# A table of places for every step of a recurrence-and-mixing kernel, and two edits to its gate arithmetic

## The chip, the cores and the metric

The kernel runs on one core of one Trainium2 chip. The metric is the device time of that core in microseconds (us), lower is better. Its engines work side by side, each through its own queue in order: TensorE (PE, with its weight loads PEld), VectorE (DVE), ScalarE (ACT), GpSimd (POOL) and SyncE (SP), which issues the DMAs.

## The reference

Two stages. The first is a complex, gated linear recurrence for 4 batches x 8 heads x 768 positions x 48 channels; the second mixes each position with the one before it and sends it through three matrix products.

```python
mag = np.sqrt(a_re * a_re + a_im * a_im)
scale = np.minimum(mag, 0.999) / (mag + 1e-06)
a_re_n, a_im_n = a_re * scale, a_im * scale
for t in range(S):                       # S_re, S_im: 48 x 48 for each batch and head
    new_re = ar * S_re - ai * S_im
    new_im = ar * S_im + ai * S_re
    S_re, S_im = new_re + k[t] v[t]^T, new_im
    y[t] = q[t] @ S_re
x_prev = x shifted by one position       # x: y with the heads side by side, 384 wide
xk = mu_k * x + (1 - mu_k) * x_prev      # xr likewise, with mu_r
k = np.maximum(xk @ w_k, 0)              # 384 -> 1024
v = k * k @ w_v                          # 1024 -> 384
out = sigmoid(xr @ w_r) * v
```

## The kernel before, in words

The work is cut into 8 units: unit `u` is one half (384 positions) of batch `u // 2`. Each unit passes three stages.

- **`gate(u)`** turns the gate into a running logarithm and a running angle. It loads `g` (the rows a_re, a_im, k, q, 128 channels at a time, three times) and `v`. `a0` takes |a_re| on ACT (line 591), a guard that sums how far a_re lies under a least value (line 595), Ln, Exp(-ln) and, on DVE, the ratio a_im / a_re (line 604). `a1` makes the logarithm of the magnitude, `a2` scans it along the positions (line 637) and multiplies k and q by its exponentials (line 654). `b0` takes the arctangent, scans the angle (line 665) and brings it to -pi..pi in a tile `r`: a product that is stored as a whole number (line 682), the remainder (685), a clamp (688) and, by clearing the sign bit, its absolute value (691). `b1` takes cosine and sine on ACT and multiplies k and q by them (line 704: "the rotations", six for a unit).
- **`attend(u)`**: PE turns the rotated k and q (line 768), forms the state's growth (789), which DVE adds up (800, 802), the scores (818), which DVE masks (823), and the values `y` (849); ACT copies from PSUM (774, 871). SP moves the rotated rows into the stacked buffers `kq` (736) and `y` into the tile `xt` (882).
- **`mix(u)`**: DVE and ACT form `xm` (348, 356) and split it into a high and a low half `x` (364, 367). PE multiplies by the weights (line 381: 3 blocks `z` for the sigmoid and 8 for w_k, of 9 matmuls each); ACT takes relu and square (418, 422), DVE splits the square (`hhi`, 426; `hlo`, 430), and PE multiplies by w_v (line 444: 8 blocks `o` of 9). DVE multiplies by the sigmoid (460).

The weights come as doubles in 10 pieces (`fetch`) and are turned into two float halves (`convert`): ACT (506, 526), four DVE steps (509, 512, 516, 520) and one POOL subtraction (529) for each piece, through two buffers `wx`.

All this is first recorded as steps and then ordered by the class `Plan`. Each recorded instruction group has an engine, a cost, what it reads and writes, and the buffer slots it uses. `Plan.run` plays a clock forward: whenever an engine is free, it takes, of the steps that are ready and whose slots are free, the one that is due first. The order so found is the order in which the program is written out, so each engine's queue is fixed when the program is built. Before, the due times come from `due`: each step is given a time (`AT_A`, `AT_M`, `AT_M0`, `DELAY`: so many units after the unit's beginning), PE's costs are summed in that order, and all else is counted back from PE.

The buffers that matter here: `g` has two (units u and u + 2 share one), `m`, `ph`, `sq`, `xk`, `xr`, `xt`, `zr` and the accumulators `o` have one, `kq` six, PSUM five blocks. The tile `r` of units 0 and 1 lies in the mixing buffer `xk` (`R_XK = 2`), that of later units in `sq`.

Of the kernel before, what the change touches and what calls it, by code (L numbers as in the profile page):

```python
# [69 lines left out]
class Plan:  # L70
# [21 lines left out]
    def op(self, engine, cost, emit, reads=(), writes=(), uses=(), table=None, heat=1.0):  # L92
# [5 lines left out]
        for k in writes:  # L98
# [12 lines left out]
    def due(self):

        ops = self.ops
        late = [math.inf] * len(ops)
        t = 0.0
        for i in sorted((i for i, o in enumerate(ops) if o["engine"] == "PE"), key=lambda i: (ops[i]["at"], i)):
            t += ops[i]["cost"]
            late[i] = t
        left = [len(f) for f in self.follow]
        due, free = [0.0] * len(ops), {}  # L120
        heap = []

        def push(i):
            late[i] = min(late[i], t + 2.0)
            heapq.heappush(heap, (-late[i], -i))
        for i, n in enumerate(left):
            if not n:
                push(i)
        while heap:
            i = -heapq.heappop(heap)[1]  # L130
            o = ops[i]
            e = o["engine"]
            s = late[i] - o["cost"]
            if e not in ("PE", "NONE"):
                s = min(late[i], free.get(e, math.inf)) - o["cost"]
                free[e] = s
                if e == "SP":
                    s -= self.START + self.ARRIVE
            due[i] = s
            for j in o["after"]:  # L140
                late[j] = min(late[j], s - self.LATENCY)
                left[j] -= 1
                if not left[j]:
                    push(j)
        return due

    def run(self):
# [33 lines left out]
        while len(order) < len(ops):  # L181
# [868 lines left out]
```

## Time and profile before

| | |
|---|---|
| time, median of 3 runs | 477.33 us (476.31 to 477.69) |
| the profiled execution's own time | 476.16 us |
| its span, first to last instruction | 474.40 us |
| instructions in the span | 12425 |
| granted TensorE clock, mean | 0.938 |
| read from HBM, written | 31.07 MB, 4.72 MB |

The profile's page gives for each engine the time in which it was busy. Its strip of 40 slices (11.9 us each) shows the busy share in tenths, and in the row PEclk the clock that TensorE was granted. The views used below are: the table of stretches (busy time of every engine between two moments), the groups of instructions by line and shape (count, total busy time, mean ns of one, then idle time before them), one line's own view (shortest, median and longest instruction), the waits (who waited for whom), and the timeline (start, duration, and in brackets the idle time before and what ended it). A group's durations overlap a little with their neighbours, so a sum of them is somewhat above busy time.

### The profile page before, as it was taken

Reading aid. Unit: us, or ns where it says so; the run is one execution under the profiler, and the core shown is the slowest. Engines: PE = TensorE matmul, PEld = TensorE weight load, DVE = VectorE, ACT = ScalarE, POOL = GpSimd, SP = SyncE. Lnnn points to the kernel's source line nnn. Section 1 sums busy time; section 2 is a strip of 40 time slices with the busy share of each in tenths; the row PEclk is TensorE's granted clock in tenths of the full one; section 3 lists DMA queues with packets and bytes.
Section 4 is the critical chain, followed back from the end, with each engine's and each line's share of the span. In section 5 each row is a group of like instructions: output and inputs, shape, how many; then the busy total and the mean of one; then the engine's idle time right before and its main releaser. Section 6 shows DMA issues by size and latency. Waiting matters only on the chain.

```text
span 474.4 us, 12425 instructions
## 1 busy us (share of the span) xinstructions
PE 382.8 (81%) x5162; PEld 351.0 (74%) x5162; DVE 374.5 (79%) x610; ACT 299.9 (63%) x498; POOL 32.3 (7%) x45
## 2 busy tenths in 40 slices
PE   0008445879966999979989999999799988999994
PEld 0006433868755999869978898999689967999993
DVE  0798999969989889898989799569967898248222
ACT  7768445597549667957894775866669753434530
POOL 4004210214210000000000000000000000000000
PEclk9999755789978999999999999999899989999998
DMA  8998154502717056416551834072523115210101
GB/s 287 409 409 142 36 184 161 123 1 52 275 26 182 21 195 203 106 51 192 181 130 61 296 102 114 34 252 100 135 78 82 45 48 137 76 35 10 51 0 57
DMA packets 25935, 60.26 MB, mean 127 GB/s; under 512 B 5392, under 2 KB 14608, under 8 KB 25872
## 3 DMA queue, kind: packets, MB, share of 16 engines
q1 hardware_dynamic: 25872, 59.40, 40.7%
q8 instruction: 42, 0.69, 0.6%
q14 instruction: 21, 0.17, 0.1%
HBM read 31.07 MB, written 4.72 MB: 75 GB/s over the span
## 4 chain that ended last, share of the span: by engine, by line
PE 42%; DVE 28%; ACT 13%; DMA 7%; issue 5%; SPq 3%; POOL 1%; DVEq 0%; ACTq 0%
PE z L381 19%; PE o L444 12%; PE y L849 5%; DVE ph L665 4%; DMA kq<-g 3%; PE sc L818 3%; DVE g L654 3%; DMA g<-in_gat 3%; SPq L736 3%; PE up L789 2%; ACT sq L264 2%; DVE m L637 2%; DVE g L704 2%; DVE xm L356 2%; ACT L261 2%
## 5 line engine op out<-in xcount | busy, mean ns | idle before, releaser
L381 PE MATMUL z<-x,w 128*128 128x384 f32 x792 | 155.9, 347 | 5.0 <-DVE state L800 1.9
L381 PEld LDWEIGHTS z<-x,w 128*128 128x128 f32 x792 | 140.3, 193 | 8.4 <-DVE state L800 2.2
L444 PE MATMUL o<-hhi,w 128*128 128x384 f32 x384 | 103.8, 353 | 1.3 <-DVE hhi L426 1.3
L444 PEld LDWEIGHTS o<-hhi,w 128*128 128x128 f32 x384 | 71.3, 196 | 3.2 <-DVE hhi L426 2.5
L444 PE MATMUL o<-hlo,w 128*128 128x384 f32 x192 | 67.9, 354 | 5.6 <-DVE hlo L430 5.5
L768 PE MATMUL tr<-ident,g 128*128 128x128 f32 (+1 forms) x144 | 27.7, 311 | 49.3 <-DVE g L704 47.8
L418 ACT ACTIVATE r<-z 128x384 f32<-128x384 f32 x64 | 31.0, 486 | 55.2 <-PE z L381 55.0
L768 PEld LDWEIGHTS tr<-ident,g 128*128 128x128 f32 (+1 forms) x144 | 17.8, 148 | 55.9 <-issue 31.9
L426 DVE CAST hhi<-h 128x384 fp32r<-128x384 f32 x64 | 22.6, 353 | 33.3 <-ACT h L422 21.2
L704 DVE TENSOR_TENSOR g<-g,r 128x768 f32<-128x768 f32 x48 | 43.7, 951 | 1.8 <-ACT r L264 1.7
L444 PEld LDWEIGHTS o<-hlo,w 128*128 128x128 f32 x192 | 37.8, 197 | 8.7 <-DVE hlo L430 8.6
L818 PE MATMUL sc<-kq 112*64 112x64 f32 x768 | 31.7, 233 | 8.9 <-DMA kq<-g 2.7
L818 PEld LDWEIGHTS sc<-kq 112*64 112x64 f32 x768 | 26.9, 144 | 15.5 <-issue 6.2
L430 DVE TENSOR_TENSOR hlo<-h,hhi 128x384 fp32r<-128x384 f32 x64 | 35.8, 559 | 1.4
L264 ACT ACTIVATE sq<-m 128x1152 f32<-128x1152 f32 (+2 forms) x27 | 28.1, 1054 | 11.1 <-DVE m L620 7.0
L364 ACT CAST x<-xm 128x384 fp32r<-128x384 f32 x48 | 24.2, 511 | 17.1 <-DVE xm L356 13.6
L422 ACT ACTIVATE h<-r 128x384 f32<-128x384 f32 x64 | 33.2, 523 | 2.5 <-DVE hlo L430 1.5
L789 PEld LDWEIGHTS up<-v,kt 64*48 64x48 f32 (+1 forms) x1408 | 27.0, 139 | 6.8 <-ACT kt L774 3.9
L849 PE MATMUL y<-kq,state 112*48 112x64 f32 (+1 forms) x704 | 25.7, 229 | 7.5 <-DVE state L800 5.1
L849 PEld LDWEIGHTS y<-kq,state 112*48 112x48 f32 (+1 forms) x704 | 23.2, 136 | 11.4 <-DVE state L800 5.3
L789 PE MATMUL up<-v,kt 64*48 64x48 f32 (+1 forms) x1408 | 29.4, 231 | 2.4 <-DVE state L800 1.3
L529 POOL TENSOR_TENSOR w<-wx,w 128x768 fp32r<-128x768 f32 (+1 forms) x10 | 24.5, 2454 | 85.6 <-ACT w L526 85.6
(74 smaller groups left out, 551.3 us busy)
## 6 DMA issues: line engine op xcount, KB each, us to landing
kq<-g SPq DMA_DIRECT2D x96, 144.0 KB, 3.2
g<-in_gat SPq DMA_DIRECT2D x18, 768.0 KB, 6.9
raw<-in_w_all SPq DMA_DIRECT2D x9, 768.0 KB, 11.6
g<-in_gat SPq DMA_DIRECT2D x12, 384.0 KB, 7.3
v<-in_vt SPq DMA_DIRECT2D x24, 192.0 KB, 4.6
out_t<-y SPq DMA_DIRECT2D x24, 192.0 KB, 2.1
xt<-ys SPq DMA_DIRECT2D x48, 72.0 KB, 2.2
kq<-g SPq DMA_DIRECT2D x32, 96.0 KB, 2.8
```

The costliest lines, as they stand in the source:

```text
L264: nc.scalar.activation(out=out, in_=in_, func=func, **kw)
L381: nc.tensor.matmul(z, lhsT=wt[s[0]][:, part, s[1]], rhs=r[which][:, ct], start=n == 0, stop=n == 3 * NT - 1)
L418: nc.scalar.activation(out=t["r", j], in_=t["f", j], func=AF.Relu)
L422: nc.scalar.activation(out=t["h", j], in_=t["r", j], func=AF.Square)
L430: nc.vector.tensor_tensor(out=t["lo", j], in0=t["h", j], in1=t["hi", j].bitcast(F32), op=ALU.subtract)
L444: nc.tensor.matmul(tiles["o", mt], lhsT=wt[W_V + 2 * j][:, part, ts(mt, P)], rhs=r, start=j == 0 and n == 0, stop=j == NJ - 1 and n == 2)
L529: nc.gpsimd.tensor_tensor(out=t["w"][:, :, 1], in0=t["x"], in1=t["w"][:, :, 0].bitcast(F32), op=ALU.subtract)
L704: nc.vector.tensor_tensor(out=g[:, ct, 2 * i:2 * i + 2], in0=g[:, ct, 2:4], in1=t["r"][:, ct, 1 - i:2 - i].to_broadcast([P, 2, U]), op=ALU ...
L768: nc.tensor.transpose(out=t["tr", c, part][:, ct * P:(ct + 1) * P], in_=G[u][:, ct, 2 * part, c * P:c * P + rows], identity=ident)
L789: nc.tensor.matmul(t["up", c, s][i * HR:(KR if i else HR), h * D:(h + 1) * D], lhsT=keys[r, i * D:(2 * D if i else HR)], rhs=V[u][c][r, h ...
L818: nc.tensor.matmul(sc[s * SB:s * SB + SB, i, c], lhsT=kq[h][:, 0, q], rhs=kq[h][:, 1, q], start=True, stop=True)
L849: nc.tensor.matmul(t["y", v][s][rows, h // 2 % 2, c], lhsT=lhsT[:, cols], rhs=rhs, start=(s, h % 2) not in begun, stop=stop)
```

## The change

It has three parts.

1. **Places instead of due times.** `Plan.due` now reads a table, `ORDER`: for each part of the work (gate, fetch, convert, attend, mix of each unit) and each engine, one number for each of its steps. Among ready steps with free slots the one with the lowest number goes first. Costs and delays of `Plan`'s clock are altered, and a slot is free only a latency after its last use. Those numbers order the program; none of them is executed.
2. **Gates without the clamped ratio.** |a_re| becomes Relu(a_re), the separate guard (line 595) is gone, and the guard's sum is instead gathered by the Exp that is there anyway. The limits of the final check are set accordingly.
3. **The tile `r`** is laid out with its two halves apart, so that each half of a unit is one run of 1152 numbers and not three runs of 384; its absolute value is taken by ACT and no longer by DVE; and unit 1's `r` lies in `sq`, not in the mixing buffer (`R_XK = 1`).

```diff
-AT_A = (0.0, 0.6)
-AT_M = (1.2, 2.1)
+ORDER = {
+    ("g", 0): dict(SP=(1, 16, 6, 15, 23, 27, 13, 8, 20,), ACT=(11, 47, 49, 61, 16, 31, 10, 45, 46, 26,), DVE=(12, 22,
+         13, 11, 8, 29, 9, 7, 33, 4,)),
...
+    ("w", 0): dict(ACT=(78,), DVE=(72,), POOL=(1,)),
...
-R_XK = 2
+R_XK = 1
...
-    def due(self):
+    def due(self, places):
+        steps = {}
+        for o in self.ops:
+            steps.setdefault((o["key"][0], o["engine"]), set()).add(o["key"][1])
+        place = {}
+        for (phase, e), s in steps.items():
+            given = places.get(phase, {}).get(e, range(len(s)))
+            place.update(((phase, e, x), n) for x, n in zip(sorted(s), given, strict=True))
+        return [place[o["key"][0], o["engine"], o["key"][1]] for o in self.ops]
...
-                    heapq.heappush(ends, (end, i))
+                    heapq.heappush(ends, (end + self.LATENCY, i))
...
-                    nc.scalar.activation(out=t["m"][:, c], in_=G[u][:, c, 0], func=AF.Abs)
-                def low():
-                    nc.scalar.activation(out=t["ph"][:, c], in_=G[u][:, c, 0], func=AF.Relu, scale=-1.0, bias=re_min,
-                                         accum_out=stat[:, i:i + 1])
+                    nc.scalar.activation(out=t["m"][:, c], in_=G[u][:, c, 0], func=AF.Relu)
...
-                op_act(n, lambda: act(t["ph"][:, c], t["m"][:, c], AF.Exp, scale=-1.0), table=(u, "exp"),
-                       reads=kk("m", c), writes=kk("ph", c), uses=[s_m, s_ph])
+                op_act(n + 110, lambda: act(t["ph"][:, c], t["m"][:, c], AF.Exp, scale=-1.0, accum_out=stat[:, i:i + 1]),
+                       table=(u, "exp"), reads=kk("m", c), writes=kk("ph", c), uses=[s_m, s_ph])
...
-                        t["r"] = (mp["x"] if u < R_XK else tp).tile([P, NT, 2, U], F32, tag="xk" if u < R_XK else "sq", name="r")
-                    t["n", c.start] = t["r"][:, c, 1].bitcast(I32)
+                        t["r"] = (mp["x"] if u < R_XK else tp).tile([P, 2, NT, U], F32, tag="xk" if u < R_XK else "sq", name="r")
+                    t["n", c.start] = t["r"][:, 1, c].bitcast(I32)
...
-                op_dve(n, lambda: nc.vector.tensor_single_scalar(
-                    out=t["n", c.start], in_=t["r"][:, c, 0].bitcast(I32), scalar=0x7FFFFFFF, op=ALU.bitwise_and),
-                    rate=2, reads=kk("r0", c), writes=kk("r1", c), uses=[s_r])
+                op_act(n, lambda: nc.scalar.activation(out=t["r"][:, 1, c], in_=t["r"][:, 0, c], func=AF.Abs),
+                       reads=kk("r0", c), writes=kk("r1", c), uses=[s_r])
```

How the queues move is seen at three places; the line numbers of the changed kernel differ from those above. The first is DVE at the start, in `gate(0)`: `m`, `ph`, `g`, `sq` and `stat` belong to the gate, `wx` and `raw` to the weights. Before:

```order
L627 TENSOR_SCALAR m<-m 128x384
L620 SCALAR_TENSOR_TENSOR m<-sq,m 128x768
L637 SCALAR_TENSOR_TENSOR m<-m,sq 128x384
L644 COPY stat<-m 128x1
L627 TENSOR_SCALAR m<-m 128x768
L646 TENSOR_SCALAR m<-m 128x384
L637 SCALAR_TENSOR_TENSOR m<-m,sq 128x384 x2
L654 TENSOR_TENSOR g<-g,sq 128x768
```

Of the change, in the same stretch of DVE's queue:

```order
L638 TENSOR_TENSOR ph<-g,ph 128x768
L671 SCALAR_TENSOR_TENSOR m<-m,sq 128x384
L550 TENSOR_SCALAR wx<-wx 128x384
L678 COPY stat<-m 128x1
L553 TENSOR_SCALAR wx<-wx 128x384
L680 TENSOR_SCALAR m<-m 128x384
L557 SCALAR_TENSOR_TENSOR wx<-raw,wx 128x384
L654 SCALAR_TENSOR_TENSOR m<-sq,m 128x768
L688 TENSOR_TENSOR g<-g,sq 128x768
L561 SCALAR_TENSOR_TENSOR wx<-raw,wx 128x384
```

The conversion of the weights' first piece has moved up between the gate's steps. Counted through DVE's whole queue, four pieces are converted before PE's first `z` block was given its last input before, and seven with the change.

The second place is ACT at the very start (`m` and `ph` of the gate, `tiny` a constant). Before:

```order
L591 ACTIVATE m<-g 128x384
L595 ACTIVATE ph,stat<-g,re_min 128x384
L261 ACT_TABLE_LOAD
L264 ACTIVATE m<-m,tiny 128x384
L591 ACTIVATE m<-g 128x768
L595 ACTIVATE ph,stat<-g,re_min 128x768
L264 ACTIVATE m<-m,tiny 128x768
L264 ACTIVATE ph<-m 128x384
```

Of the change:

```order
L632 ACTIVATE m<-g 128x384
L304 ACT_TABLE_LOAD
L307 ACTIVATE m<-m,tiny 128x384
L307 ACTIVATE ph,stat<-m 128x384
L650 ACTIVATE sq,stat<-ph 128x384
L632 ACTIVATE m<-g 128x768
```

The first third of the gate (128x384) now goes ahead of the other two (128x768), and the guard's instructions are gone.

The third place is DVE where the last unit is rotated (`g_3826` before and `g_3787` after are unit 7's tile; `hhi` and `hlo` belong to the mixing of unit 5, `pt` to the scores, `xm` and `x` to the mixing of unit 6). Before:

```order
L688 TENSOR_SCALAR r_4691<-r_4691 128x3x384
L430 TENSOR_TENSOR hlo_4724<-h_4671,hhi_4708 128x384
L691 TENSOR_SCALAR r_4691<-r_4691 128x3x384
L426 CAST hhi_4738<-h_4693 128x384
L367 TENSOR_TENSOR x_4673<-xm_4621,x_4673 128x384
L430 TENSOR_TENSOR hlo_4742<-h_4693,hhi_4738 128x384
L356 SCALAR_TENSOR_TENSOR xm_4744<-dx_4639,mu_sb_81,xt_4325 128x384
L704 TENSOR_TENSOR g_3826<-g_3826,r_4691 128x768
L426 CAST hhi_4758<-h_4726 128x384
L704 TENSOR_TENSOR g_3826<-g_3826,r_4691 128x768
L430 TENSOR_TENSOR hlo_4765<-h_4726,hhi_4758 128x384
L704 TENSOR_TENSOR g_3826<-g_3826,r_4691 128x768 x4
```

Of the change:

```order
L722 TENSOR_SCALAR r_4482<-r_4482 128x1152
L467 CAST hhi_4533<-h_4460 128x384
L471 TENSOR_TENSOR hlo_4536<-h_4460,hhi_4533 128x384
L737 TENSOR_TENSOR g_3787<-g_3787,r_4482 128x768
L467 CAST hhi_4565<-h_4502 128x384
L737 TENSOR_TENSOR g_3787<-g_3787,r_4482 128x768
L856 TENSOR_TENSOR pt_4581<-sc_4552,mask_71 128x384
L471 TENSOR_TENSOR hlo_4583<-h_4502,hhi_4565 128x384
L737 TENSOR_TENSOR g_3787<-g_3787,r_4482 128x768 x2
L467 CAST hhi_4637<-h_4632 128x384
L737 TENSOR_TENSOR g_3787<-g_3787,r_4482 128x768
```

The absolute value (line 691) has left DVE, one row of `x` and three of `xm` fewer stand ahead of the last rotation, and 45 instead of all 48 `hlo` steps of units 0 to 5.

More of the change, by code (lines that the diff above doesn't have):

```diff
@@ L102, in op, with steps, run @@
         self.ops.append(dict(engine=engine, cost=cost, emit=emit, after=after - {None, i}, uses=uses,
-                             at=self.at, table=table, heat=heat))
-    def steps(self, steps, a, b):
+                             key=self.key, table=table, heat=heat))
+    def steps(self, steps, phase):
         for i, f in enumerate(steps):
-            self.at = a + (b - a) * (i + 0.5) / len(steps)
+            self.key = phase, (i + 0.5) / len(steps)
             f()
-    def due(self):
[L113 to L147, printed above, removed]
+    def due(self, places):
[7 more added lines that the diff above has]
+        return [place[o["key"][0], o["engine"], o["key"][1]] for o in self.ops]
+    def run(self, places):
         ops = self.ops
@@ L225, in run @@
                         free[e] = end
-                    for at in (free[e], end):
+                    for at in (free[e], end + self.LATENCY):
                         heapq.heappush(events, at)
-                    heapq.heappush(ends, (end, i))
+                    heapq.heappush(ends, (end + self.LATENCY, i))
                     for j in self.follow[i]:
@@ L236, in run @@
                     o["start"], o["end"], o["on"], o["took"] = t, end, e, o["cost"]
-        self.length = end
+        self.length = max(o["end"] for o in ops)
         for i in order:
@@ L398, in out_ @@
                 nc.scalar.copy(out=zr[u][:, mt], in_=tiles["z", mt])
-            op_pe(1.58, mul, reads=parts(1) + [("w", W_R + ct) for ct in range(NT)], writes=[("z", u, mt)],
+            op_pe(1.62, mul, reads=parts(1) + [("w", W_R + ct) for ct in range(NT)], writes=[("z", u, mt)],
                   uses=[sp, part_slot[1]])
@@ L445, in mul @@
                                          start=j == 0 and n == 0, stop=j == NJ - 1 and n == 2)
-            op_pe(1.58, mul, reads=[("hhi", u, j), ("hlo", u, j), ("w", W_V + 2 * j)] + [("o", u, j - 1)] * (j > 0),
+            op_pe(1.62, mul, reads=[("hhi", u, j), ("hlo", u, j), ("w", W_V + 2 * j)] + [("o", u, j - 1)] * (j > 0),
                   writes=[("o", u, j)], uses=[so, *hs[j]])
@@ L774, in f1 @@
                         nc.scalar.copy(out=t["kt", c][:rows, :, part], in_=t["tr", c, part].rearrange("p (h d) -> p h d", d=D))
-                    op_pe(0.35, f0, heat=0.5, reads=[("kqs" if part else "kqc", u, ct) for ct in range(NT)],
+                    op_pe(0.41, f0, heat=0.8, reads=[("kqs" if part else "kqc", u, ct) for ct in range(NT)],
                           writes=[("tr", u, c, part)], uses=[sp, sk, g_slot[u]])
@@ L917, in tile_kernel @@
         n = range(len(pieces))
-        run(gate(0) + [lambda i=i: fetch(i) for i in n] + [lambda i=i: convert(i) for i in n] + gate(1), 0, 0)
+        run(gate(0), ("g", 0))
+        for i in n:
+            run([lambda i=i: fetch(i)], ("f", i))
+        for i in n:
+            run([lambda i=i: convert(i)], ("w", i))
+        run(gate(1), ("g", 1))
         for u in range(NU):
-            t = u + DELAY if u else 0
-            run(attend(u), t + AT_A[0], t + AT_A[1])
-            a, e = AT_M if u else AT_M0
-            run(mix(u), t + a, t + e)
+            run(attend(u), ("a", u))
+            run(mix(u), ("m", u))
             if u + 2 < NU:
-                run(gate(u + 2), 0, 0)
+                run(gate(u + 2), ("g", u + 2))
         with tc.manual_schedule():
-            plan[0].run()
+            plan[0].run(ORDER)
     bad = keep.tile([1, 1], I32, name="bad")
@@ L1010, in tile_kernel @@
                 zr.clear()
-                plan[0].steps(mix(u), 0, 1)
-                plan[0].run()
+                plan[0].steps(mix(u), ("m", u))
+                plan[0].run({})
 def kernel(q, k, v, a_re, a_im, moe_mu_k, moe_mu_r, moe_w_k, moe_w_v, moe_w_r):
```

112 lines of the change are left out of this document (86 added, 26 removed).

## The prediction

> **What bounds the kernel now.** I read the page's strip first, then cut the span into stretches by what PE does, then looked at the waits inside each. In the strip a digit is the busy share of 11.9 us in tenths.
>
> ```profile
> PE   0008445879966999979989999999799988999994
> DVE  0798999969989889898989799569967898248222
> PEclk9999755789978999999999999999899989999998
> ```
>
> The order of saturation is the point: DVE is full from the second slice on while PE is empty or half idle until about slice 13; from slice 32 on PE is full and DVE falls off. The stretches (columns: length, then busy us of PE, PEld, DVE, ACT, POOL, then the granted clock, the DMA engines' share and their GB/s) are cut at PE's first transpose, its first `z` block, the transposes of unit 2 and the end of the dense part:
>
> ```profile
> 0.00:31.70 31.70, 0.00 (x0) 0.03 (x1) 17.87 (x33) 21.22 (x34) 5.73 (x21) 1.00 0.95 365
> 31.70:88.30 56.60, 30.57 (x649) 24.82 (x649) 55.10 (x76) 33.56 (x52) 9.50 (x5) 0.73 0.54 151
> 88.30:141.80 53.50, 45.34 (x461) 41.33 (x461) 47.36 (x68) 34.97 (x55) 15.20 (x6) 0.87 0.29 91
> 141.80:320.00 178.20, 167.95 (x2505) 155.01 (x2506) 153.54 (x258) 131.77 (x219) 0.87 (x2) 0.99 0.47 141
> 320.00:400.00 80.00, 71.09 (x917) 64.33 (x916) 70.40 (x116) 52.37 (x88) 0.26 (x1) 0.96 0.33 88
> 400.00:442.00 42.00, 42.00 (x486) 40.23 (x485) 21.24 (x45) 16.36 (x36) 0.77 (x10) 1.00 0.19 58
> 442.00:474.40 32.40, 25.85 (x150) 25.25 (x148) 8.99 (x20) 9.68 (x18) 0.00 (x0) 0.94 0.06 21
> ```
>
> Up to 88.3 DVE sets the pace (55.10 of 56.60 in the second row). From 88.3 to 141.8 the two alternate. From 141.8 to 442 PE does: it idles 178.20 - 167.95 + 80.00 - 71.09 = 19.2 us, and the clock below 1.00 costs it about 0.01 x 168 + 0.04 x 71 = 4.5 us. The last row is the end of unit 7, where nothing is left to overlap. What PE waits for:
>
> ```profile
> 88.34 9.58 PE L381 MATMUL z<-x,w 128*128 128x384 f32 x45 [1.90 <-DVE state L800]
> 141.86 0.33 PE L768 MATMUL tr<-ident,g 128*128 128x128 f32 x1 [0.96 <-DVE g L704]
> 212.37 1.38 PE L849 MATMUL y<-kq,state 112*64 112x64 f32 x40 [2.41 <-ACT zr L398]
> 336.73 0.66 PE L768 MATMUL tr<-ident,g 128*128 128x128 f32 x4 [1.68 <-DVE g L704]
> ```
>
> Late rotations of a unit (line 704) and ACT held at the `zr` copies are the two kinds that recur.
>
> **The edits to the operations.** The groups that they touch (count, then busy us and mean ns):
>
> ```profile
> L682 DVE TENSOR_SCALAR r<-ph 128x1152 int32<-128x1152 f32 x7 | 9.4, 1347 | 0.1
> L682 DVE TENSOR_SCALAR r<-ph 128x768 int32<-128x768 f32 x1 | 0.6, 552 | 0.0
> L688 DVE TENSOR_SCALAR r<-r 128x1152 f32<-128x1152 f32 x7 | 6.7, 950 | 0.0
> L691 DVE TENSOR_SCALAR r<-r 128x1152 int32<-128x1152 int32 x7 | 6.6, 949 | 0.0
> L646 DVE TENSOR_SCALAR m<-m 128x1152 f32<-128x1152 f32 x7 | 5.3, 754 | 0.1
> L691 DVE TENSOR_SCALAR r<-r 128x768 int32<-128x768 int32 x1 | 0.5, 549 | 0.0
> L591 ACT ACTIVATE m<-g 128x1152 f32<-128x1152 f32 x7 | 8.1, 1161 | 0.0
> L595 ACT ACTIVATE ph<-g,re_min 128x1152 f32<-128x1152 f32 x7 | 8.8, 1254 | 1.9 <-DVE stat L674 1.9
> L616 ACT ACTIVATION_READ_ACCUMULATOR sq<-ph 128x1 f32 x9 | 1.7, 189 | 0.0
> ```
>
> DVE loses line 691: 0.95 us in each of units 1 to 7, about 0.9 in unit 0 (0.55 for its two thirds), 7.5 in all. Lines 682 and 688 work on three runs of 384 and take 1347 and 950 ns; line 646 does the like on one run of 1152 in 754, and line 682 itself takes 552 for two runs. Laid flat, 682 and 688 should cost 754: 0.59 + 0.20 = 0.8 us in each of 7 units, 5.6 in all. Bounds: nothing (the conversion to whole numbers keeps its 1347), and 5.6. I take 5.6, since the 768 form converts too and is fast. The page "VectorE: DVE Perf Modes" of the Trainium skill (What auto-detection actually checks) gives the doubled rate where a single source and the destination have outermost dimensions both even or equal. For 688 these are equal (3 and 3), so by that rule it would already be fast and only 682 would gain: 4.1 instead of 5.6. The trace disagrees for 688 (950 against 754), and the trace decides.
>
> ACT loses line 595 (7 x 1.25, by its size some 1.5 in unit 0, and nine accumulator reads of 0.19: 12 us) and gains an absolute value, which I price as the one in line 591 (7 x 1.16 + 1.3 = 9.4), and nine reads behind the Exp (1.7). Net -0.9, beside other work, since ACT is at most three quarters busy in any stretch after the first. On a unit's own chain the step is dearer by 1.16 - 0.95 = 0.2 us, and it now waits for whatever ACT has ahead of it. Where DVE sets the pace, another of its steps fills that wait; later, the cover is PE's other work. If both fail, each unit pays up to one relu and one square ahead of it, about 1 us.
>
> `R_XK = 1` moves unit 1's `r` out of `xk` into `sq`:
>
> ```profile
> 79.21 0.95 DVE L704 TENSOR_TENSOR g<-g,r 128x768 f32<-128x768 f32 x1
> 81.73 0.55 DVE L367 TENSOR_TENSOR x<-xm,x 128x384 fp32r<-128x384 f32 x1
> 101.89 1.15 ACT sq L616 x2
> ```
>
> Unit 0's low halves are first written at 81.73, when unit 1's last rotation (until 80.16) is over and has freed `xk` anyway: no gain. Unit 2's `sq`, first written at 101.89 (third row, from the chain of waits), must now wait for that same end: no loss. Zero on both sides; if unit 2's gate came 20 us earlier it would begin to cost. The altered costs of `Plan` are no instructions.
>
> **The moves, stretch by stretch.** First, up to the first `z` (88.3). DVE began late and a weight piece costs it four steps:
>
> ```profile
> 10.71 0.56 DVE L604 TENSOR_TENSOR ph<-g,ph 128x384 f32<-128x384 f32 x1 [9.75 <-ACT ph L264]
> 5.17 0.60 ACT L595 ACTIVATE ph<-g,re_min 128x384 f32<-128x384 f32 x1
> 7.17 0.61 ACT L264 ACTIVATE m<-m,tiny 128x384 f32<-128x384 f32 x1
> 10.17 1.24 ACT L264 ACTIVATE ph<-m 128x384 f32<-128x384 f32 x2
> L509 DVE TENSOR_SCALAR wx<-wx 128x768 f32<-128x768 f32 x9 | 4.9, 545 | 5.2 <-ACT wx L506 5.2
> L512 DVE TENSOR_SCALAR wx<-wx 128x768 int32<-128x768 int32 x9 | 4.9, 548 | 0.0
> L516 DVE SCALAR_TENSOR_TENSOR wx<-raw,wx 128x768 int32<-128x768 int32 x9 | 9.7, 1080 | 0.0
> L520 DVE SCALAR_TENSOR_TENSOR wx<-raw,wx 128x768 int32<-128x768 int32 x9 | 8.5, 947 | 0.0
> ```
>
> A piece is 0.55 + 0.55 + 1.08 + 0.95 = 3.1 us. Ahead of the first `z` stood four pieces and five steps of two more; now seven and two steps: three pieces more and three steps (2.2) less, +7 us. Taken off: line 691 of units 0 and 1 and the flat layout of unit 1, -2.6. Filled: the 9.75 us of idle shrink by some 3, as the first Exp (10.17) can follow its Ln (7.17 to 7.78, and 0.6 sooner without the guard) and no longer waits behind the other two thirds; and steps of the first pieces stand in the gate's holes, 1 us: -4. Added: POOL's subtraction, which goes along with each piece:
>
> ```profile
> L529 POOL TENSOR_TENSOR w<-wx,w x10: 1829/2213/4377, 39.6 to 131.3; 128x768 fp32r<-128x768 f32 x9, 128x384 fp32r<-128x384 f32 x1
> L627 DVE TENSOR_SCALAR m<-m x9: 361/747/1964, 13.8 to 365.0; 128x1152 f32<-128x1152 f32 x7, 128x384 f32<-128x384 f32 x1, 128x768 f32<-128x768 f32 x1
> ```
>
> (shortest/median/longest ns.) The longest 627 falls while POOL subtracts, and loses 1.96 - 0.75 = 1.2 us; I count 1.3 for a meeting. Two more ahead of `z`: +2.6. Sum: 7 - 2.6 - 4 + 2.6 = **+3** (bounds -2, all weights in idle time, and +6, none). SP's queue: the loads of unit 1's `g` are now dealt out among the weights and two late pieces (8, 9) are fetched before others; a piece of 0.79 MB at the 365 GB/s of the first row is 2.2 us, so a late one holds ACT by 2 to 4 us. The rows of ACT that need them stand several us later; inside the bounds.
>
> Second, 88.3 to 141.8. Of the weights there remained four pieces and three steps for DVE (12.4 + 3.0 us), now two pieces and two steps (6.2 + 2.0): -7. Line 691 and the flat layout of unit 2: -1.75. Three meetings with POOL fewer: -4. That is -12.7 on DVE, of which PE allows -10: its 45.34 us of work at a clock of 0.87 need 43.8 at 0.90. **-10** (bounds -4, -14). The page "TensorE: Matmul & The Clock Gate" of the Trainium skill (Part 1) has only half and full speed, with full speed after one busy window of about 3.4 us. By that rule an unbroken stretch would run at full clock: 39.4 us, 4 less than I take.
>
> Third, 141.8 to 442. The edits alone take 7.5 + 5.6 = 13.1 us out of DVE ahead of unit 7's last rotation and the order moves six more behind it (three `hhi`/`hlo` pairs of 0.9, and `x` steps of 0.6). What that reaches is the stretch 320 to 400, where DVE is 88% busy with the gates of units 6 and 7 and PE idles 8.9 us, on rotations (336.73, above) and on the splits that queue among them:
>
> ```profile
> 381.32 0.44 PE L444 MATMUL o<-hlo,w 128*128 128x384 f32 x1 [1.11 <-DVE hlo L430]
> 389.26 0.44 PE L444 MATMUL o<-hlo,w 128*128 128x384 f32 x1 [0.71 <-DVE hlo L430]
> ```
>
> Most of these waits should go. What comes late next, the `kq` moves or the state, has to fit the idle that I leave. I let idle fall from 19.2 to 8 and the clock's loss from 4.5 to 2: **-14** (bounds -21, +4). The `zr` waits I leave as they are. The last 32.4 stay.
>
> Sum on the span: 474.4 + 3 - 10 - 14 = 453.4. The profiled execution took 476.16, 1.8 more than its span, and the median is 1.2 above that: 453.4 + 3.0, about 456; as the -14 leans on my own choice of what idle remains, I round to **455 us**, 4.7% less.
>
> **Rivals.** (a) PE never waits once `z` has begun: 88.3 + 3 + 39.4 + (281 - 4.5) + 32.4 = 439.6, with 3.0 about **443**. For it: DVE has slack (245 of 300 us after 141.8). Against: all gates wait on single buffers. 12%. (b) The second stretch's gain is given back: gates of later units are tied to buffers `g` and `kq` that come free at PE's pace, so after 88.3 only the edits tell, 1.75 us in each of four units' chains: 474.4 + 3 - 7 + 3.0, about **473**. 9%. (c) Slower: ACT's fixed queue. A `zr` copy must wait for the unit before to be multiplied out, here for the third product `y` (the row of ACT names the small copy that follows it on DVE):
>
> ```profile
> 211.22 0.53 DVE L460 TENSOR_TENSOR y<-o,zr 128x384 f32<-128x384 f32 x1
> 211.84 1.24 ACT L398 COPY zr<-z 128x384 f32<-128x384 f32 x3 [3.23 <-DVE stat L644]
> ```
>
> Behind it stand the Exps that DVE's scan needs and the relus that free PSUM; PE lost 2.41 us to it at 212. Now Abs stands in that queue too, and `zr` copies are dealt out singly. If each of units 2 to 7 met such a stop and lost 3.2 + 2.4 us more, 34 us are added: 453 + 34 + 3 = **490**. It decides above 4 us a unit. 7%. (d) The table changes little, as slots are taken in order whatever the number: only the edits count, about 473; the moved rows speak against it. 2%.
>
> **Numbers.** 70% for the forecast. Its own range is 440 to 471 (-22 to +4 on the stretches that were chosen). The range 440 to 473 takes in most of (a) and all of (b), and leaves out (c) and the forecast's own edges, some 0.15 together. A measurement tells 0.3% (1.4 us): faster 0.89, same 0.03, slower 0.08.
>
> **What would show it.** Right: the first `z` between 86 and 94 us; unit 2's first transpose at 130 to 138; lines 682 and 688 near 0.75 us for 1152; PE idle after that under 12 us, none of it on unit 7's rotations. Wrong: `z` after 97, PE idle above 19, or ACT waiting at `zr` copies over 3 us in several units.

## The result, and the profile after

The changed kernel takes **461.13 us** (median of 4 runs, 460.63 to 461.86) against 477.51 us before (4 runs, 476.31 to 477.97): a ratio of 0.966, 95% interval 0.9639 to 0.9684, 3.4% faster. The forecast was 455 us within 440 to 473. Its profiled execution took 460.97 us, with a span of 459.3 us.

The strip of the page after, in slices of 11.5 us:

```profile
PE   0004851699876899999989997999999998999994
DVE  1999999999799896897998878996889775239323
PEclk9999976599998999999999998999999999999999
```

VectorE now works in the first slice (1 for 0). PE starts later (its fourth digit is a 4 where an 8 stood) and has its thin slices, 5 1 6, later too; but from slice 9 on it is fuller, and no digit of the clock after the eighth is under 8. The stretches, cut at the same events as before (first transpose, first `z`, unit 2's transposes, the end of the dense part; the same columns):

```profile
0.00:37.90 37.90, 0.05 (x1) 0.08 (x1) 26.70 (x44) 25.35 (x39) 9.05 (x22) 1.00 0.87 343
37.90:95.50 57.60, 33.76 (x708) 28.43 (x708) 54.90 (x74) 39.11 (x59) 11.99 (x6) 0.76 0.47 135
95.50:135.70 40.20, 37.06 (x407) 33.71 (x403) 37.67 (x56) 27.74 (x46) 8.51 (x3) 1.00 0.31 105
135.70:320.00 184.30, 170.19 (x2521) 158.30 (x2522) 159.41 (x268) 139.46 (x227) 0.69 (x2) 0.98 0.49 145
320.00:400.00 80.00, 77.97 (x1127) 72.62 (x1126) 59.83 (x109) 48.59 (x89) 0.19 (x1) 1.00 0.31 83
400.00:427.00 27.00, 27.00 (x257) 26.20 (x256) 15.67 (x34) 9.73 (x22) 0.70 (x10) 1.00 0.14 45
427.00:459.30 32.30, 26.45 (x153) 25.85 (x151) 8.99 (x20) 9.81 (x19) 0.00 (x0) 0.98 0.07 23
```

The first `z` comes at 95.5 us instead of 88.3 (+7.2). From there to unit 2's first transpose it takes 40.2 us instead of 53.5 (-13.3). From that transpose to the end it takes 323.6 us instead of 332.6 (-9.0). The three add up to the span's -15.1.

The groups that were edited, after (count, then busy us, mean ns):

```profile
L716 DVE TENSOR_SCALAR r<-ph 128x1152 int32<-128x1152 f32 x7 | 5.3, 752 | 0.0
L722 DVE TENSOR_SCALAR r<-r 128x1152 f32<-128x1152 f32 x7 | 5.3, 753 | 0.0
L725 ACT ACTIVATE r<-r 128x1152 f32<-128x1152 f32 x7 | 8.2, 1167 | 9.2 <-DVE r L722 9.2
```

Lines 716 and 722 (682 and 688 before) cost what was forecast for the flat layout, and line 725 what was forecast for ScalarE's absolute value. VectorE is busy for 363.2 us where it was for 374.5.

What PE still waits for between unit 2's first transpose and the end of the dense part (us in all, times, longest):

```profile
PE tr L801 <- DVE g L737: 3.9, 5, 2.3
PE sc L851 <- ACT r L459: 2.3, 1, 2.3
PE up L822 <- ACT kt L807: 2.0, 3, 0.9
...
PE z L422 <- ACT zr L439: 1.1, 1, 1.1
```

Before, between the same two events, these rows stood for the rotations and the splits:

```profile
PE tr L768 <- DVE g L704: 6.5, 8, 1.7
PE o L444 <- DVE hlo L430: 1.8, 2, 1.1
PE o L444 <- DVE hhi L426: 1.1, 3, 0.6
```

By the windows PE idles there for 14.1 + 2.0 + 0 = 16.1 us, against 19.2 before. The waits for `hlo` and `hhi` are gone, the late rotations fell from 6.5 to 3.9 us, and in their place stand many single waits of 1 to 2 us, each on something else.

### The profile page after: what moved, and what is told of

It reads as the page before. It is cut to its first block, busy times and chain, and to the rows that moved or that the text cites. A ratio compares the mean times of both kernels' runs of the same rounds, so it can differ in the third digit from the quotient of the medians.

```text
span 459.3 us, 12409 instructions
## 1 busy us (share of the span) xinstructions
PE 372.5 (81%) x5162; PEld 345.2 (75%) x5162; DVE 363.2 (79%) x601; ACT 299.8 (65%) x498; POOL 31.1 (7%) x44
## 4 chain that ended last, share of the span: by engine, by line
PE 48%; DVE 23%; ACT 10%; DMA 9%; issue 6%; SPq 3%; DVEq 0%; ACTq 0%
PE z L422 19%; PE o L485 12%; PE y L882 5%; PE up L822 5%; PE sc L851 4%; DVE g L737 3%; DMA g<-in_gat 3%; DMA v<-in_vt 3%; DVE ph L699 3%; PE tr L801 2%; DVE wx L557 2%; DVE m L671 2%; SPq L769 2%; ACT r L307 1%; DVE g L688 1%
## 5 line engine op out<-in xcount | busy, mean ns | idle before, releaser
L422 PE MATMUL z<-x,w 128*128 128x384 f32 x792 | 152.1, 342 | 2.7 <-DVE pt L856 1.6
L422 PEld LDWEIGHTS z<-x,w 128*128 128x128 f32 x792 | 137.7, 190 | 4.5 <-DVE pt L856 1.8
L485 PE MATMUL o<-hhi,w 128*128 128x384 f32 x384 | 101.0, 344 | 0.1
L485 PEld LDWEIGHTS o<-hhi,w 128*128 128x128 f32 x384 | 67.9, 189 | 1.7 <-DVE hhi L467 0.6
L485 PE MATMUL o<-hlo,w 128*128 128x384 f32 x192 | 65.7, 342 | 2.4 <-DVE hlo L471 2.3
L737 DVE TENSOR_TENSOR g<-g,r 128x768 f32<-128x768 f32 x48 | 47.0, 1019 | 2.7 <-ACT r L307 2.7
L822 PEld LDWEIGHTS up<-v,kt 64*64 64x64 f32 (+1 forms) x1408 | 26.9, 140 | 10.0 <-ACT kt L807 5.1
L822 PE MATMUL up<-v,kt 64*64 64x48 f32 (+1 forms) x1408 | 29.2, 232 | 5.5 <-ACT kt L807 3.1
L397 DVE SCALAR_TENSOR_TENSOR xm<-dx,mu_sb,xt 128x384 f32<-128x384 f32 x48 | 28.6, 612 | 0.2
L408 DVE TENSOR_TENSOR x<-xm,x 128x384 fp32r<-128x384 f32 x48 | 25.9, 552 | 3.5 <-ACT x L405 3.2
```

What stands on the lines that cost most here:

```text
L397: nc.vector.scalar_tensor_tensor(out=xm[which, ct], in0=d[ct], scalar=mu_sb[:, which, ct:ct + 1], in1=X[u][:, ct, 0:U], op0=ALU.mult, op1= ...
L408: nc.vector.tensor_tensor(out=lo[which][:, ct], in0=xm[which, ct], in1=hi[which][:, ct].bitcast(F32), op=ALU.subtract)
L422: nc.tensor.matmul(z, lhsT=wt[s[0]][:, part, s[1]], rhs=r[which][:, ct], start=n == 0, stop=n == 3 * NT - 1)
L485: nc.tensor.matmul(tiles["o", mt], lhsT=wt[W_V + 2 * j][:, part, ts(mt, P)], rhs=r, start=j == 0 and n == 0, stop=j == NJ - 1 and n == 2)
L737: nc.vector.tensor_tensor(out=g[:, ct, 2 * i:2 * i + 2], in0=g[:, ct, 2:4], in1=t["r"][:, 1 - i, ct:ct + 1].to_broadcast([P, 2, U]), op=AL ...
L822: nc.tensor.matmul(t["up", c, s][i * HR:(KR if i else HR), h * D:(h + 1) * D], lhsT=keys[r, i * D:(2 * D if i else HR)], rhs=V[u][c][r, h ...
```

## The experiments

The kernel before was run again beside these kernels and took 476.8 to 477.7 us (medians); the intervals are of the ratio to it, and the change's own is 0.9639 to 0.9684. Each kernel computes everything. Three theories stood at first: the new operations and the new places share the gain, as the prediction's sum had it (A); the places give it all (B); the operations give it all (C).

**1. The operations alone, planned by the old rules** (`e1_edits_only`): the kernel before with the new a0, b0, b1 and limits, `R_XK = 1`, and its own `due`.

> The kernel before with the edits of the operations alone (gates without the guard, r laid flat with its absolute value on ACT, R_XK = 1) and the old due times. Theory A (both parts pay, the edits where DVE sets the pace, the places for the rest): 468 to 474 us. Rival B (the places are all of it, the edits are off the path): 476 to 478. Rival C (the edits are all of it): 460 to 463.

Measured: 457.45 us, ratio 0.957 (0.952 to 0.9629). All ranges were missed on the fast side: without the table it is 3.7 us faster than the change itself. What follows: the operations together with the old rules give more than the change does. But the old rules plan a new order for new operations, so this is not the operations alone.

**2. The places alone** (`e2_places_only`): the changed kernel with the old operations and `R_XK = 2`.

> The changed kernel with the operations of before (guard, old layout of r, absolute value on DVE, R_XK = 2) and the table of places. Theory A: 465 to 471 us. Rival B: 460 to 463. Rival C: 475 to 479.

Measured: 489.09 us, ratio 1.024 (1.018 to 1.0304), slower than the kernel before. All ranges were missed. The table is made of numbers for one set of operations; with another set, steps come ready at other times and the same numbers give another order (experiment 7, with the same operations in the change's own order and `R_XK = 1`, is 17 us faster). The first transpose, at 46.8 us, waits all that time for unit 0's rotation (the wait of PE in that kernel):

```profile
PE tr L811 <- DVE g L747: 73.2, 7, 46.8
```

So neither 1 nor 2 holds the order still, and they can't be subtracted from each other. Experiment 4 meets the same trap.

**3. The old layout of `r`, same order** (`e3_old_layout`):

```diff
-t["r"] = ....tile([P, 2, NT, U], F32, ...)
+t["r"] = ....tile([P, NT, 2, U], F32, ...)
```

> The changed kernel with r again in three runs of 384; the rest unchanged. Lines 716 and 722 go back to about 1.35 and 0.95 us for 1152, 5.6 us more on DVE. Theory A: 1 to 4 us slower than the changed kernel, 462 to 465. Rival (PE sets the pace, DVE's 5.6 us are hidden): within 1 us of it.

Measured: 464.46 us, ratio 0.973 (0.9652 to 0.981), 3.3 us over the change for 5.1 us more of VectorE. That is theory A's range, but a rough size: the runs spread from 461.8 to 467.9, and the interval overlaps the change's. In that kernel the two lines cost (shortest, median, longest ns):

```profile
L716 DVE TENSOR_SCALAR r<-ph x9: 346/1344/1347, 31.2 to 356.7; 128x1152 int32<-128x1152 f32 x7, 128x384 int32<-128x384 f32 x1, 128x768 int32<-128x768 f32 x1
L722 DVE TENSOR_SCALAR r<-r x9: 345/950/959, 33.4 to 359.8; 128x1152 f32<-128x1152 f32 x7, 128x384 f32<-128x384 f32 x1, 128x768 f32<-128x768 f32 x1
```

The layout alone makes 1344 and 950 out of 752 and 753 ns; the first `z` stays at 95.5, and the loss comes after it.

**4. The absolute value planned on VectorE** (`e4_abs_on_dve`): in b0 `op_act(... AF.Abs)` becomes `op_dve(... bitwise_and)`, and the table deals out the places again.

> The changed kernel with the absolute value of r back on DVE, in the flat layout (0.75 us a unit on DVE, 9.4 us less on ACT). Theory A (DVE's time counts): 0 to 3 us slower than the changed kernel. Rival (the hand-over to ACT's queue costs more than the step saves): 1 to 3 us faster.

Measured: 485.35 us, ratio 1.014 (1.0074 to 1.0214), 24 us over the change; no theory had that. Unit 1's rotations then begin at 86.3 us instead of 76.7, scores wait for the `kq` moves, and in VectorE's timeline steps of the first mix stand among those rotations, with long meetings ahead of them (instructions that run beside a subtraction of POOL's, and take longer):

```profile
PE sc L852 <- DMA kq<-g: 32.8, 5, 19.1
```

```profile
66.63 5.97 DVE L699 TENSOR_TENSOR_SCAN ph<-ph,stat,zero 128x384 f32<-128x384 f32 x3
...
82.25 4.15 DVE L397 SCALAR_TENSOR_TENSOR xm<-dx,mu_sb,xt 128x384 f32<-128x384 f32 x2
86.33 0.94 DVE L738 TENSOR_TENSOR g<-g,r 128x768 f32<-128x768 f32 x1
```

One step that changes its engine gave another order. The step itself is priced in 5: 3.3 of the 24 us. From here on the order is held: each step is planned as what it was and only what it issues is changed.

**5. The absolute value on VectorE, order held** (`e7_abs_same_order`): still planned by `op_act`, but issued as

```diff
-nc.scalar.activation(out=t["r"][:, 1, c], in_=t["r"][:, 0, c], func=AF.Abs)
+nc.vector.tensor_single_scalar(out=t["n", c.start], in_=t["r"][:, 0, c].bitcast(I32), scalar=0x7FFFFFFF, op=ALU.bitwise_and)
```

> The changed kernel with the order of all its steps kept as it is, and only the absolute value (line 725) done by VectorE (the bit mask, 0.75 us for 1152) where ScalarE does it now (1.17 us). It differs from e4_abs_on_dve in that nothing is planned anew. Theory A (VectorE's relief is what counts, about 0.65 us of time for each us of VectorE, as the old layout showed: 5.1 us for 3.3): 5.8 us more on VectorE, 2 to 5 us slower than the change, 463 to 466 us; the 24 us of e4 were the other order that the table gives when one step changes its engine. Rival R (the absolute value on ScalarE is itself worth that much, since it lets VectorE go on in the rotation): 475 to 485 us, with PE idle over 30 us after the first z.

Measured: 464.47 us, ratio 0.9725 (0.9685 to 0.9766), 3.3 us over the change: theory A. With the same operations experiment 4 is 20.9 us slower, so 21 of its 24 us were the order.

**6. New operations in the old order** (`e8_new_ops_old_order`): the kernel before, all steps planned as before, the new operations issued (the guard's step issues nothing; the absolute value goes to ScalarE at the place that it had). `R_XK` stays 2 here, and 1 in experiment 7: it goes with the order.

> The kernel before with the order of its steps kept as it was planned for the old operations, and only the operations made new (no guard relu, Relu for Abs in line 591, the sum behind the Exp, flat r, the absolute value on ScalarE at the place that it had). It differs from e1_edits_only in that nothing is planned anew (and in R_XK, which stays 2). Theory A (the operations give the gain by themselves): 457 to 463 us, first z at 86 to 89, VectorE's busy time down by 11 to 13 us. Rival B (they give it because the order is planned for them): 467 to 474 us.

Measured: 469.26 us, ratio 0.983 (0.979 to 0.9869): rival B. The operations by themselves give 7.7 us; the other 12 of experiment 1 come from the old rules planning anew for them. Its windows (to the first transpose, the first `z`, unit 2, the end):

```profile
0.00:31.20 31.20, 0.00 (x0) 0.02 (x1) 17.22 (x31) 21.09 (x34) 5.69 (x20) 1.00 0.95 372
31.20:86.60 55.40, 31.82 (x649) 25.95 (x649) 53.66 (x75) 33.97 (x52) 9.61 (x5) 0.72 0.55 154
86.60:139.30 52.70, 43.30 (x461) 39.35 (x461) 46.93 (x67) 34.98 (x55) 15.72 (x6) 0.90 0.29 92
139.30:467.90 328.60, 304.21 (x4052) 283.46 (x4052) 246.28 (x431) 210.03 (x360) 2.19 (x13) 0.98 0.37 107
```

**7. Old operations in the new order** (`e9_old_ops_new_order`): the changed kernel, all steps planned as there, the old operations issued.

> The changed kernel with the order of all its steps kept, and the old operations in it (guard relu, Abs, no sum behind the Exp, r in three runs of 384, the absolute value on VectorE at the place that ScalarE's has). It differs from e2_places_only in that nothing is planned anew for them. Theory A (operations alone): the change's 461 plus what the old layout (3.3) and the absolute value on VectorE (2 to 5) cost, and the guard's 10 us of ScalarE at little: 466 to 473 us. Rival B (the order is worth much by itself): below 466. Rival C (an order planned for one set of operations falls apart with the other): 480 to 490, as e2 was.

Measured: 472.21 us, ratio 0.988 (0.983 to 0.9923): theory A's range. The same windows:

```profile
0.00:40.90 40.90, 0.05 (x1) 0.08 (x1) 27.46 (x46) 27.57 (x43) 9.09 (x23) 1.00 0.82 317
40.90:100.00 59.10, 33.83 (x708) 28.35 (x708) 56.48 (x75) 38.29 (x56) 16.05 (x6) 0.68 0.45 132
100.00:141.70 41.70, 37.19 (x405) 33.72 (x403) 39.20 (x57) 27.99 (x48) 8.51 (x3) 1.00 0.30 101
141.70:472.30 330.60, 308.51 (x4052) 289.12 (x4052) 251.92 (x435) 206.47 (x353) 1.49 (x13) 0.97 0.36 107
```

With the old operations, then, the new order puts the first `z` 11.7 us later and gets 11.8 us back by unit 2's first transpose: 141.7 us, where the kernel before has 141.8. With the new operations it puts the first `z` 8.9 us later and gets 12.5 back: 135.7 us, where experiment 6 has 139.3. Experiments 6 and 7 with the two kernels make a square of stretches in profiled spans (us):

| | to the first `z` | to unit 2 | to the end | span |
|---|---|---|---|---|
| old operations, old order | 88.3 | 53.5 | 332.6 | 474.4 |
| new operations, old order | 86.6 | 52.7 | 328.6 | 467.9 |
| old operations, new order | 100.0 | 41.7 | 330.6 | 472.3 |
| both: the change | 95.5 | 40.2 | 323.6 | 459.3 |

In medians the operations give 7.7, the order 4.8, and both 16.4: 3.9 us more than the two by themselves.

**8. The first part in the old rules' order** (`e10_first_part_old`): new operations; the first 297 steps as in experiment 1, all others in the order of the table.

```diff
+        if places:
+            order = list(FIRST) + [i for i in order if i not in FIRST]
```

> The new operations; the first 297 steps in the order of e1_edits_only (old due times: what starts up to about the first z), all others in the order of the change's table. e1's first z came 8.1 us earlier than the change's, and the change made 4.2 us of it good between the first z and the transposes of unit 2. Theory D (what the table gains after the first z is only the weights that it has done ahead): 456 to 460 us, no better than e1, as the weights that are left now stand in that stretch. Rival E (the table's later part is better by itself): 449 to 454 us.

Measured: 463.73 us, ratio 0.973 (0.9681 to 0.9773), somewhat over theory D's range; rival E is out. The first transpose comes at 31.2 us (30.7 in experiment 1), but the first `z` only at 99.3, since the weight steps that the table had put earlier are now the next in line, and unit 2 starts at 140.1. Work that leaves one side of the first `z` turns up on the other.

**9. One weight piece put behind the first `z`** (`e13_piece_behind`): piece 6, and 9 a little later.

```diff
+        if places:
+            at = {i: n for n, i in enumerate(order)} | MOVED
+            order.sort(key=at.get)
```

> The changed kernel with one of the seven weight pieces that stand ahead of the first z (number 6, first needed 17 us after it) put behind the first z, and number 9 a little later for it; all else in the same order. Theory Z (moving weight work across the first z is paid back one for one, as VectorE is the limit on both sides): the first z 3 to 5 us earlier, at 91 to 93; unit 2's first transpose within 1.5 us of 135.7; 460 to 463 us. Rival E (PE's earlier start is kept): unit 2's first transpose at 131 to 133, 456 to 459 us. Rival L (pieces behind the first z hold PE's products up): over 464 us.

Measured: 462.55 us, ratio 0.969 (0.964 to 0.9747): inside theory Z's range, with the first `z` at 91.9 us (3.6 earlier) and unit 2 at 137.6 (1.9 later, 0.4 more than was allowed). The interval overlaps the change's. Its windows around that point:

```profile
37.60:91.90 54.30, 30.66 (x708) 25.37 (x708) 50.45 (x70) 37.56 (x57) 10.55 (x5) 0.75 0.51 143
91.90:137.60 45.70, 39.50 (x406) 35.98 (x403) 37.88 (x60) 29.52 (x48) 9.58 (x4) 0.93 0.27 92
```

**10. The guard relu back, order held** (`e14_guard_back`): ahead of line 632, with its sum there.

```diff
+nc.scalar.activation(out=t["ph"][:, c], in_=G[u][:, c, 0], func=AF.Relu, scale=-1.0, bias=re_min, accum_out=stat[:, i:i + 1])
```

> The changed kernel, same order, with the guard relu back ahead of line 632 on ScalarE (and its sum there instead of behind the Exp). Old operations in the new order cost 11.1 us more than the change (e9_old_ops_new_order); the old layout explains 3.3 of them and the absolute value on VectorE 3.3. Theory G (effects add up: ScalarE's queue, not VectorE alone, sets what a gate takes, and the guard's 10 us on ScalarE are worth the other 4.5): 464 to 467 us. Rival P (as the prediction priced it: ScalarE has room, so that the guard costs only the 0.6 us by which the first Exp comes later): 461 to 462.5 us, and the three old operations cost more together than one by one.

Measured: 467.0 us, ratio 0.977 (0.9742 to 0.9806), 5.9 us over the change: theory G. Some of it is not the guard itself. ScalarE's first table load in that kernel stands behind the wait for `g`, while in the change it runs from 0.82 to 2.10 us, before `g` lands. The rows of experiment 10's kernel:

```profile
4.68 1.28 ACT L634 ACT_TABLE_LOAD   x1 [4.68 <-DMA g<-in_gat]
5.98 0.61 ACT L634 ACTIVATE ph<-g,re_min 128x384 f32<-128x384 f32 x1
...
9.06 0.52 ACT L307 ACTIVATE ph<-m 128x384 f32<-128x384 f32 x1
```

Of the 2.0 us by which the first Exp comes later (7.08 in the change), 1.3 are that load. The first `z` is 2.9 us later, unit 2 3.9. With the layout's 3.3 and the absolute value's 3.3 the three come to 12.5 one by one, and to 11.1 together (experiment 7), so the three nearly add up.

**11. The weights' low halves on VectorE instead of POOL, order held** (`e11_low_on_dve`): line 570, `nc.gpsimd` becomes `nc.vector`.

> The changed kernel, same order, with the weights' low halves (line 570) subtracted by VectorE instead of POOL. In the change's trace VectorE's instructions that ran beside POOL's subtraction ahead of the first z were 8.2 us longer than the same forms elsewhere; on VectorE a subtraction of 768 should take about 0.95 us (the rotation's 768 form takes 0.95 to 1.02), 6.2 us ahead of the first z. Theory M (the meetings hold VectorE up by what the rows show): the first z 1 to 4 us earlier, 458 to 462 us in all. Rival N (POOL's work lies beside VectorE's at next to nothing): the first z 4 to 7 us later, 464 to 470 us.

Measured: 456.96 us, ratio 0.959 (0.9543 to 0.9643), theory M, and 1 us beyond its range: 4.2 us faster than the change, with ten more instructions on VectorE and the first `z` at 91.2 us. Its four runs spread from 453.5 to 459.4, and the profiled one is the lowest. The scans of lines 671 and 699 (shortest, median, longest ns), first in the change, then here:

```profile
L671 DVE TENSOR_TENSOR_SCAN m<-m,sq x12: 925/946/2558, 13.6 to 294.7; 128x384 f32<-128x384 f32 x12
L699 DVE TENSOR_TENSOR_SCAN ph<-ph,stat,zero x12: 987/1012/2520, 65.0 to 352.4; 128x384 f32<-128x384 f32 x12
```

```profile
L671 DVE TENSOR_TENSOR_SCAN m<-m,sq x12: 931/946/958, 13.1 to 286.5; 128x384 f32<-128x384 f32 x12
L699 DVE TENSOR_TENSOR_SCAN ph<-ph,stat,zero x12: 992/1009/1018, 63.1 to 344.3; 128x384 f32<-128x384 f32 x12
L570 DVE TENSOR_TENSOR w<-wx,w x10: 528/944/958, 19.4 to 108.3; 128x768 fp32r<-128x768 f32 x9, 128x384 fp32r<-128x384 f32 x1
```

No instruction is stretched any more, and VectorE is busy for 358.1 us in all, 5.1 less than in the change, though it does 0.53 + 9 x 0.94 = 9.0 us more.

**12. The same in experiment 1** (`e12_edits_low_on_dve`).

> e1_edits_only (457.5 us), same order, with the weights' low halves on VectorE. There POOL is busy for 36.2 us. Theory M: as much or more is freed as is added, 454 to 458 us, which would be the fastest version so far. Rival N: 461 to 467 us.

Measured: **452.81 us** (452.71 to 453.25), ratio 0.949 (0.9451 to 0.9531): 1.2 us under theory M's range and the fastest version, 8.3 us under the change, with the old rules and no table.

```profile
30.70:86.90 56.20, 32.84 (x677) 27.12 (x677) 54.87 (x81) 41.08 (x62) 0.28 (x1) 0.73 0.58 167
86.90:128.30 41.40, 38.96 (x434) 36.24 (x435) 38.99 (x63) 27.14 (x44) 0.00 (x0) 0.95 0.29 96
128.30:451.00 322.70, 304.01 (x4052) 285.94 (x4052) 247.17 (x435) 208.26 (x359) 1.51 (x13) 0.98 0.38 110
```

It has both ends: the first `z` at 86.9 us, earlier than the kernel before, and unit 2 at 128.3, 7.4 earlier than the change.

## Why the prediction was right, and where not

The direction and the size hold: 461.1 against 455, 16.4 us gained where 22.5 were forecast. By stretches the forecast was +3, -10, -14 and 0, and the trace has +7.2, -13.3, -9.0 with the end's 32.3 us unchanged. That the first two come out together nearly as forecast is in part luck, since their errors, +4.2 and -3.3, cancel. The upper end of the range, 473, is not the sum of the stretches' own bounds: they add up to 440 at the one end and to 483 at the other.

**First stretch (+3 forecast, +7.2 measured, beyond the bound of +6).** VectorE's work ahead of the first `z` grew by 26.70 + 54.90 - 17.87 - 55.10 = 8.6 us, where the terms 7 - 2.6 + 2.6 made 7. The term that failed more is the -4 for idle time filled: VectorE's idle there is 13.9 us instead of 15.3, so 1.4 was filled. Its first step of the gate came 3.0 us earlier, as forecast, but new gaps stand behind it:

```profile
7.72 0.56 DVE L638 TENSOR_TENSOR ph<-g,ph 128x384 f32<-128x384 f32 x1 [6.77 <-ACT ph L307]
10.64 0.56 DVE L654 SCALAR_TENSOR_TENSOR m<-sq,m 128x384 f32<-128x384 f32 x1 [2.36 <-ACT sq L307]
11.88 0.36 DVE L661 TENSOR_SCALAR m<-m 128x384 f32<-128x384 f32 x1 [0.68 <-ACT sq L307]
```

The meetings with POOL were priced rightly and counted wrongly. I took two more at 1.3 us each. Three more of VectorE's instructions were stretched (six; three in the kernel before), and they ran 8.0 us over the same forms elsewhere instead of 4.2: 3.8 more, 1.3 each. These rows of VectorE's timeline are groups that ran beside a subtraction of POOL's:

```profile
18.97 2.55 DVE L671 TENSOR_TENSOR_SCAN m<-m,sq 128x384 f32<-128x384 f32 x2
27.02 4.21 DVE L699 TENSOR_TENSOR_SCAN ph<-ph,zero 128x384 f32<-128x384 f32 x3
47.45 2.30 DVE L654 SCALAR_TENSOR_TENSOR m<-sq,m 128x1152 f32<-128x1152 f32 x1
64.97 4.36 DVE L699 TENSOR_TENSOR_SCAN ph<-ph,stat,zero 128x384 f32<-128x384 f32 x3
76.71 6.83 DVE L737 TENSOR_TENSOR g<-g,r 128x768 f32<-128x768 f32 x4 [0.71 <-ACT r L307]
```

Against the same rows of the kernel of experiment 11 (0.95 for one scan, and 5.29 for six rotations, 0.88 each) they are 0.7, 1.5, 0.95, 1.5 and 3.3 us too long, some 8 us. The last row met two subtractions, and taken apart it shows how the engines meet:

```profile
77.48 1.89 POOL L570 TENSOR_TENSOR w<-wx,w 128x768 fp32r<-128x768 f32 x1 [9.87 <-ACT w L567]
77.59 2.59 DVE L737 TENSOR_TENSOR g<-g,r 128x768 f32<-128x768 f32 x1
79.32 2.55 POOL L570 TENSOR_TENSOR w<-wx,w 128x768 fp32r<-128x768 f32 x1
80.10 2.58 DVE L737 TENSOR_TENSOR g<-g,r 128x768 f32<-128x768 f32 x1
```

Each rotation begins while a subtraction runs, and ends 0.8 us after it, at 80.18 and 82.68 us: about the time that a free rotation takes, 0.95.

**Second stretch (-10 forecast, -13.3 measured).** VectorE lost 47.36 - 37.67 = 9.7 us of work there where I counted 12.7. The missing 3 us are the term of -4 for three meetings fewer: the stretched instructions cost 4.8 us there after and 5.7 before, so it is worth -0.9. PE allowed more than I let it: the granted clock is 1.00 and not the 0.90 that I took, and 54 matmuls of the 461 now run ahead of `z`. The clock rule of the Trainium skill's page "TensorE: Matmul & The Clock Gate" (Part 1: full speed after a busy window) would have given 39.4 us; the trace has 40.2 at a clock of 1.00, so here the rule was the better price, and my middle value the wrong step. That the two come so close is in part luck: PE's work was 37.06 us, 2.3 less than 39.4, as fewer matmuls were left, and it idled for 3.1 us.

**The moves.** The prediction saw the weights' +7 and -7 as a zero, and took its gain in the first two stretches from filled idle time, POOL and the edits: -7 net, against -6.1 measured. Up to unit 2's first transpose VectorE's idle time fell from 21.5 to 16.4 us: 5.0, where 4 were forecast, but only 1.4 of it ahead of the first `z`. The meetings went the other way: the forecast's +2.6 and -4 make -1.4, and they rose by 3.0, from 9.9 to 12.9 us. The square shows the order's part. With the old operations it fills 2.9 us of VectorE's idle time by unit 2 (21.5 to 18.6), adds 2.8 us of busy time, and gains 0.1. With the new ones it fills 5.1 (21.5 to 16.4), adds 1.5, and gains 3.6. With the order held, the operations bring 2.5 us by unit 2 in the old order and 6.0 in the new (141.7 to 135.7). Up to 1.3 of the 6.0 is the late table load of experiment 10, which experiment 7 has too; it would go from the one side to the other. In experiments 8 and 9, which deal the weights' steps out otherwise, unit 2 starts at 140.1 and 137.6 us with 21.3 and 22.5 us of VectorE's idle time ahead of it: what sets them apart from the change is idle time.

**The edits.** VectorE's 13.1 us were nearly right: with the order held its busy time falls by 11.9, from 375.1 in experiment 7 to 363.2. The guard was the mis-priced edit. I took ScalarE's -0.9 as lying beside other work, worth the 0.6 by which the first Exp comes sooner; it is worth up to 5.9, or some 4.6 if the late table load's 1.3 passes through whole (experiment 10). ScalarE is at most three quarters busy, but the guard stands first in every unit's gate, and each gate is one long chain on single buffers; that this is the reason was argued, not shown. By unit 2's first transpose 3.9 us are lost. Where along the later units the rest is lost wasn't traced further.

**Third stretch (-14 forecast, -9.0 measured, inside the bounds).** The mechanism was right: unit 7's rotations end at 366.6 us instead of 392.7, none of PE's waits stand on them, and PE idles 2.0 us between 320 and 400 where it idled 8.9. The size failed in the step "most of these waits should go": idle fell from 19.2 to 16.1, not to 8, as units 2 to 5 got new waits of 1 to 2 us. The clock's loss fell by less than the 2.5 I took: PE had a clock of 0.50 in three windows of 3.4 us there before and in two after, and worked for 10.0 and 6.1 us of them, so by an estimate from these it lost 5.0 and 3.1 us, 1.9 less. These two explain 5.0 of the 9.0. PE's busy time for the same 4058 matmuls (from unit 2's first transpose to the end) fell by another 3.3 us, and its idle time at the end by 0.7; that remainder is open.

**The rivals.** (a) PE does wait. (b) and (d): the operations by themselves give 469 us, near the 473 said there, but the order is worth 4.8 alone and 8.1 with them, so the table does matter. (c) ScalarE stood at a `zr` copy for VectorE's `y` only twice, 3.8 us at the longest, and PE lost 1.1 us to it in all (the last row of its waits above).

**The signs.** Unit 2's first transpose (135.7) and the 0.75 us of the two lines came as said. The first `z` fell between the marks for right (94) and for wrong (97), and PE's idle time between 12 and 19.

**What no theory had.** The table is not what makes the change good: the old rules, planning for the same operations, are 3.7 us faster (ratios 0.957 against 0.966, their intervals apart). Of their 20 us, 7.7 are the operations and 12 the order planned for them. They finish five weight pieces ahead of the first `z` (at 87.4 us), where the change has seven, and reach unit 2 at 131.8, 7.5 us before experiment 6, whose operations are the same. Most of that is idle time filled: VectorE idles 15.0 us up to there, against 21.5 in experiment 6 and 16.4 in the change. Why the old rules find the better order here stays open.

## What to carry to other kernels

Where one engine is the limit on both sides of a point, moving its work across that point is an exchange by itself. What shortens the sum is work taken away, idle time filled, and instructions that are no longer stretched; add up each of the three on both sides of the point. To price one operation in a planned kernel hold the order still and change only what is issued: the same step cost 24 us planned anew and 3.3 us held. An engine that helps the limiting one can hold it up more than it takes off; try the work on the limiting engine itself.

## What the runs showed of the hardware

- Ten subtractions on POOL stretched VectorE's instructions by 14 us in all: its busy time fell by 5.1 us when it took over 9.0 us of work from POOL (experiment 11). A scan of 0.95 us took up to 2.56, and POOL's own subtraction 1.3 to 4.0 us where VectorE needs 0.53 or 0.94. In the change nine of VectorE's instructions are stretched, by 0.7 to 1.7 us, and the others keep their time. All nine began while a subtraction ran, and each ran over by 0.1 to 0.2 us less than what was left of that subtraction: in these meetings VectorE waited for POOL. The Trainium skill's page "SBUF — State Buffer" (SBUF: two separate sides) says that VectorE, with two inputs in SBUF or in a two-port mode, and GpSimd share a pair of ports as an exclusive lock, and that the later one waits for the whole instruction. The trace agrees for VectorE, by the nine. What made some of POOL's own subtractions longer than others (1.8 to 4.0 us for 128x768) wasn't traced.
- Three runs of 384 against one of 1152 in a one-source VectorE operation: 950 against 753 ns for fp32 to fp32, and 1344 against 752 ns where one run is read and three are written as int32 (experiment 3).
- A table load can stand behind the wait for data: ScalarE's first ran at 0.82 us in the change, and at 4.68 us, behind the load of `g`, where another activation stood first (experiment 10).
